# Slots of 1024 rows in the middle chunks of a convolution with a routed feed-forward network

## The chip, the cores and the metric

One core of one Trainium2 chip runs the kernel. The metric is the device time of one execution in microseconds (us); the median of three runs of the kernel before is 1307.97 us, with 1307.63 and 1311.01 as the others.

## The reference

```python
w = softmax(weight)                                  # 8 heads x 7 taps
x = causal convolution of x[8, 3584, 192] along the sequence, 24 columns per head
logits = x @ w_gate + modality_bias[modality_id]     # 28672 rows, 8 experts
e = argmax(logits, axis=1);  gate = softmax(logits)[e]
out[row] = gate * (relu(x[row] @ w1[e]) @ w2[e])     # w1 192x1024, w2 1024x192
```

With the inputs given, the rows go to three of the eight experts: 14239 to expert 6, 13901 to expert 7, 532 to expert 1.

## The kernel before, in words

The rows are worked off in two streams that run beside each other.

**Groups.** Nineteen groups (1, 1, 2, 2, 2 and then fourteen times 4 quads of 448 rows) are convolved, gated and sorted by expert. `convolve` (L264) multiplies with band matrices on TensorE (PE) and copies the result into one of four y buffers (two of them for a group of 4 quads); `turn`, `part_turned`, `gate`, `logits` and `choose` (L294 to L359) make the logits and the choice; `place` (L361) computes each row's place in a list of its expert in DRAM (`routed_rows`); `send` and `scatter` (L390, L210) write the rows there by one indirect DMA per 112 rows, issued by GpSimd (POOL). In `choose`, an iota on POOL (L357) writes the rows' own numbers into column 1 of y, so it has to wait until the earlier scatters out of that y buffer have landed. The first five groups (8 quads, 32 scatters) come before any expert work: this is the head.

**Slots.** A slot is a piece of one expert's list: 512 rows, or 256 in the last chunk. `Slot.__init__` (L605) loads the expert's weights on SyncE's (SP's) queue unless they are the same as two slots ago, `split` (L646, helper L98) turns them into a high and a low part, eight parts per slot, each with one copy on ScalarE (ACT, L99) and one subtraction on VectorE (DVE, L100). `bring` (L625) loads the slot's rows into one of two buffers. A pass is 256 rows: `turn` (L656) transposes them; four steps follow, each with `first` (L678, ten matmuls, relu on ACT and DVE) and, two steps later, `second` (L693, sixteen matmuls); `put` (L716) scales the result into two `o` tiles on DVE and scatters them to `out` by two indirect DMAs on POOL (L723). There are `OUTS` = 5 `o` buffers.

**Order.** `run` (L810) writes the order out by hand: step by step it emits `first`, `second`, some of the parts into which the group work is cut (as many as `due`, L775, asks for), a piece of the slot table of the next chunk, the loads and the splits of the next slot (eight parts over the eight steps of a slot). A chunk's slots may start only when its groups have been sent, and `due` aims at eleven steps before that. ACT keeps exactly this order; on the other engines a scheduler moves instructions that its model sees ready. There are 4 + 7 x 7 slots of 512 rows and a last chunk of up to 21 slots of 256, of which 8 always run: 61 slots, 114 passes, 456 steps. Before the last table is made, `fill` (L590) writes rows of zeros behind each expert's list, and `make_filler` (L580) writes the dummy list at the start, by DMAs on the ACT queue.

Of the kernel before, what the change touches and what calls it, by code (L numbers as in the profile page):

```python
# [9 lines left out]
F32 = mybir.dt.float32  # L10
# [16 lines left out]
WARM = 50  # L27
WARM2 = 0
WAIT = 3
OUTS = 5  # L30
PIN = 18
AHEAD = 26
T = 256
GROUPS_OF_CHUNK = (5, 2, 2, 2, 2, 2, 2, 2, 0)
SLOTS_OF_CHUNK = (4, 7, 7, 7, 7, 7, 7, 7)
PASSES_OF_SLOT = (2, 2, 2, 2, 2, 2, 2, 2, 1)
LEAD = 11
TURN = 1
LAG = 2
# [4 lines left out]
def conv_then_routed_ffn(ctx, tc, x, weight, modality, w_gate, mod_bias, w1, w2, out):  # L44
# [15 lines left out]
    W = D + OVER  # L60
    WIDE = max(PASSES_OF_SLOT)
    TW = WIDE * T
    CAP = N + TW
    DUMMY = E * CAP
    assert NJ == 2 and NG == sum(GROUPS_OF_CHUNK) and sum(QUADS_OF_GROUP) == 2 * NSB and NB == 8 and DB == 64 and CAP < 32768 and N % TW == 0
# [142 lines left out]
        return y_bufs[turns["y"] % 4]  # L208

    def scatter(chunk, idx, src):  # L210
        routed(chunk, nc.gpsimd.indirect_dma_start(  # L211
            out=scr, out_offset=bass.IndirectOffsetOnAxis(ap=idx, axis=0), in_=src, in_offset=None,
        ).ins)

    def routed(chunk, ins):
        for c in range(chunk + 1):
# [5 lines left out]
    class Group:  # L222
# [109 lines left out]
        def choose(self):  # L332

            n = self.tiles
            lg = self.lg

            def per_tile(ap):
                return ap.unsqueeze(2).broadcast_to([MB, n, E])

            top = rt.tile([MB, NT], F32, name="top")[:, 0:n]  # L340
            nc.vector.tensor_reduce(out=top, in_=lg, axis=AX.X, op=ALU.max)
            ex = rt.tile([MB, NT, E], F32, name="ex", bufs=1)[:, 0:n]
            nc.vector.tensor_tensor(out=ex, in0=lg, in1=per_tile(top), op=ALU.subtract)
            nc.scalar.activation(out=ex, in_=ex, func=AF.Exp)
            self.oh = rt.tile([MB, NT, E], BF16, name="oh")[:, 0:n]
            rk = rt.tile([MB, NT, E], F32, name="rk", bufs=1)[:, 0:n]
            nc.vector.tensor_tensor(out=rk, in0=lg, in1=per_tile(top), op=ALU.is_equal)
            nc.vector.tensor_tensor(out=rk, in0=rk, in1=ramp.unsqueeze(1).broadcast_to([MB, n, E]), op=ALU.mult)
            first = rt.tile([MB, NT], F32, name="first")[:, 0:n]
            nc.vector.tensor_reduce(out=first, in_=rk, axis=AX.X, op=ALU.max)  # L350
            nc.vector.tensor_tensor(out=self.oh, in0=rk, in1=per_tile(first), op=ALU.is_equal)
            den = rt.tile([MB, NT], F32, name="den")[:, 0:n]
            nc.vector.tensor_reduce(out=den, in_=ex, axis=AX.X, op=ALU.add)
            nc.vector.tensor_scalar(out=den, in0=den, scalar1=1e-9, scalar2=None, op0=ALU.add)
            for i, y in enumerate(self.ys):
                nc.vector.reciprocal(out=y[0:MB, 0:self.nb, 0], in_=den[:, i * self.nb:(i + 1) * self.nb])
                nc.gpsimd.iota(y.bitcast(I32)[0:MB, 0:self.nb, 1], pattern=[[S, self.nb]],  # L357
                               base=self.b0 * S + (self.block + i) * MB + MB - 1,
                               channel_multiplier=-1)  # L359

        def place(self):  # L361

# [117 lines left out]
    def init_tables():  # L480
        base0 = const.tile([1, E], F32, name="base0")
        nc.vector.tensor_copy(out=base0, in_=carry[0:1, :])
        done = const.tile([1, E], F32, name="done0")
        nc.vector.memset(done, 0.0)
        n_max = sum(n for _, n, *_ in plan)
        slot = const.tile([1, n_max], F32, name="slot")
        nc.gpsimd.iota(slot, pattern=[[1, n_max]], base=0, channel_multiplier=0,
                       allow_small_or_imprecise_dtypes=True)
        eid = const.tile([1, E], F32, name="eid")
        nc.gpsimd.iota(eid, pattern=[[1, E]], base=0, channel_multiplier=0,  # L490
                       allow_small_or_imprecise_dtypes=True)
        one8 = const.tile([1, E], F32, name="one8")
        nc.vector.memset(one8, 1.0)
        used = const.tile([1, n_max + 2], F32, name="used")
        nc.vector.memset(used[:, 0:2], -1.0)
        state.update(base0=base0, done=done, slot=slot, eid=eid, one8=one8, used=used)

    def table(chunk):

        s0, n, size = plan[chunk]  # L500
        last, down = chunk == len(plan) - 1, chunk % 2 == 1
        carry = state["carry"] if last else state["end", chunk]

        def small(name, shape=(1, E), dtype=F32):
            return rt.tile(list(shape), dtype, name=name, bufs=1)

        def wide(name):
            return rt.tile([1, n, E], F32, name=name, bufs=1)

        V = nc.vector  # L510
# [32 lines left out]
        V.tensor_tensor(out=past, in0=cmp, in1=state["eid"].unsqueeze(1).broadcast_to([1, n, E]), op=ALU.mult)  # L543
        used = state["used"]
        V.tensor_reduce(out=used[:, s0 + 2:s0 + 2 + n], in_=past, axis=AX.X, op=ALU.add)
        yield

        off = small("off")
# [10 lines left out]
        yield  # L559
        tab = rt.tile([1, n, 3], I32, name="tab")  # L560
        V.tensor_scalar(out=tab[:, :, 0], in0=row, scalar1=float(DUMMY), scalar2=None, op0=ALU.add)
        V.tensor_copy(out=tab[:, :, 1], in_=used[:, s0 + 2:s0 + 2 + n])
        V.tensor_tensor(out=past[:, :, 0], in0=used[:, s0 + 2:s0 + 2 + n], in1=used[:, s0:s0 + n], op=ALU.not_equal)
        V.tensor_tensor(out=tab[:, :, 2], in0=past[:, :, 0], in1=live, op=ALU.mult)
        yield
# [36 lines left out]
    class Slot:  # L602


        def __init__(self, i, chunk, ent):  # L605
            self.i, self.h, self.passes = i, {}, plan[chunk][2] // T
            self.chunk, self.ent, load = chunk, ent, nc.sync
            with tc.issue_after(state["load"]) if "load" in state else nullcontext():
                e = load.value_load(ent[:, 1:2], min_val=0, max_val=E - 1)
# [12 lines left out]
            if i > 0:  # L622
                load_second()

        def bring(self):  # L625
            chunk, size = self.chunk, plan[self.chunk][2]
            with tc.issue_after(state["load"]):
                r0 = nc.sync.value_load(self.ent[:, 0:1], min_val=0, max_val=DUMMY)
            self.rows = ring(sp, 2, [P, WIDE * NJ, W - DB], F32, "rows")[:, 0:size // P]
            self.ends = ring(sp, 2, [P, WIDE, NJ, DB], F32, "ends")[:, 0:size // T]  # L630
            src = scr[bass.ds(r0, size), :].rearrange("(j p) w -> p j w", p=P)
            for dst, part in ((self.rows, src[:, :, 0:W - DB]), (self.ends.rearrange("p k j d -> p (k j) d"), src[:, :, W - DB:W])):
# [9 lines left out]
            if self.i == 0:  # L642
                with tc.issue_after(ld):
                    self.load_second()

# [8 lines left out]
                split(w2b[i][:, cs, 0:D], w2b[i][:, cs, D:2 * D], raw2[i][:, cs, :])  # L654

        def turn(self, k):  # L656
            rows = self.rows[:, k * NJ:(k + 1) * NJ, :]
# [3 lines left out]
            nc.tensor.transpose(out=tp[:, NJ, :], in_=self.ends[:, k].rearrange("p j d -> p (j d)"), identity=ident)  # L661
# [107 lines left out]
    for c in range(1, last):  # L769
        steps += plan[c - 1][1] * steps_of(c - 1)  # L770
        g = sum(GROUPS_OF_CHUNK[:c + 1])
        marks.append((steps - LEAD, head + sum(parts_of(i) for i in range(FIRST, min(g + 1, NG)))
                      + (WAIT + 2 + 4 * QUADS_OF_GROUP[-1] if g == NG else 0)))

# [24 lines left out]
                pass  # L799
            made.append(Slot(len(made), chunk, tables[chunk][:, k, :]))  # L800

    def bring(i):

        make(i)
        while state["brought"] <= i:
            through("groups", order[state["brought"]][0])
            made[state["brought"]].bring()
            state["brought"] += 1

    def run(i0, i1):  # L810

        lagging, count = [], 0
        for i in range(i0, i1):
# [3 lines left out]
            for step in range(steps):  # L817
# [12 lines left out]
                if chunk < last and state["placed"] >= sum(GROUPS_OF_CHUNK[:chunk + 2]) and \  # L830
                        (chunk + 1 < last or state["groups"] == NG):
                    next(prepared.setdefault(chunk + 1, prepare(chunk + 1)), None)
                if steps == 4:
                    if step == 0:
                        bring(min(i + 2, i1 - 1))
                elif step == 0:
                    bring(min(i + 1, i1 - 1))
                    if i > i0:
                        make(min(i + 2, i1 - 1))
                elif step >= 4:  # L840
                    ahead = min(i + 2, i1 - 1)
                    if len(made) > ahead and state["groups"] >= sum(GROUPS_OF_CHUNK[:order[ahead][0] + 1]):
                        bring(ahead)
                    elif i == i0:
                        make(ahead)
                if i + 1 < i1:
                    if late:
                        parts = range(2 * step - 8, 2 * step - 6) if step >= 4 else ()
# [12 lines left out]
    def start(i):  # L861
        if i == 0:
            through("groups", 0)
            w2b.append(const.tile([P, NF, 2 * D], F32R, name="w2b1"))
        bring(i)
# [44 lines left out]
```

## Time and profile before

| | kernel before |
|---|---|
| median of three runs | 1307.97 us |
| the profiled execution | 1306.6 us |
| its span in the trace | 1304.9 us |
| PE / weight loads (PEld) / DVE / ACT / POOL busy | 1253.3 / 1222.3 / 1074.7 / 785.0 / 525.4 us |
| TensorE clock granted, mean | 0.983 |

The trace's times count from the span's start. The matmul times of the trace overlap one another, so a sum over a line is more than the engine's busy time; where matmuls follow one another without a gap, their starts tell how long one takes. Weight loads alternate with matmuls, and a stretch in which PEld is busy throughout is one in which PE is fed.

### The profile page before, as it was taken

How to read it: one execution, taken by the hardware profiler on the slowest of the kernel's cores; microseconds unless marked ns; L12 is line 12 of the kernel's file. 1: busy time of each engine (PE TensorE's matmuls, PEld its weight loads, DVE VectorE, ACT ScalarE, POOL GpSimd, SP SyncE). 2: the span in 40 equal slices, each digit the busy share in tenths (PEclk: the TensorE clock that was granted, in tenths of full speed). 3: DMA queues.
4: the chain of work that ended last, by engine and by line, in shares of the span. 5: the costliest groups of instructions: out<-in, count | busy, mean ns of one | idle time of the engine just before them, and what ended most of it. 6: DMA issues, size and time to landing. Idle time of an engine off the chain costs nothing.

```text
span 1304.9 us, 27875 instructions
## 1 busy us (share of the span) xinstructions
PE 1253.3 (96%) x9448; PEld 1222.3 (94%) x9448; DVE 1074.7 (82%) x2576; ACT 785.0 (60%) x1828; POOL 525.4 (40%) x574
## 2 busy tenths in 40 slices
PE   8549999999999999999999999999999999999997
PEld 7338899999999999999999999999999999999996
DVE  6459978798889888898889988898888878777895
ACT  2126566566666566766666566666665556555674
POOL 4636753442626244362624435262532612112121
PEclk9859999999999999999999999999999999999999
DMA  5467432352326241453215432352223525353440
GB/s 164 148 172 208 130 117 59 92 151 81 86 65 166 80 116 51 122 157 94 75 45 161 114 96 76 92 158 83 60 61 91 146 67 109 80 156 114 129 117 18
DMA packets 155356, 140.41 MB, mean 108 GB/s; under 512 B 43714, under 2 KB 141627, under 8 KB 155204
## 3 DMA queue, kind: packets, MB, share of 16 engines
q1 hardware_dynamic: 130164, 93.58, 27.3%
q0 software_dynamic: 23232, 44.30, 10.7%
q8 instruction: 76, 1.25, 0.4%
q10 hardware_dynamic: 1808, 0.66, 0.2%
q14 instruction: 76, 0.62, 0.2%
HBM read 160.37 MB, written 48.25 MB: 160 GB/s over the span
## 4 chain that ended last, share of the span: by engine, by line
PE 80%; issue 7%; DVE 6%; POOL 3%; DMA 2%; ACT 1%; POOLq 0%; DVEq 0%; ACTq 0%
PE hps L686 35%; PE po L704 23%; PE po L708 11%; PE cv L274 5%; PE gt L318 3%; POOL routed_rows L211 2%; PE tp L660 1%; DMA routed_rows<-y,idx 1%; POOL out_dram L723 1%; DVE hl L690 1%; PE hps L114 1%; PE tp L661 1%; DMA out_dram<-o,tag 1%; DVE turned L298 1%; DVE gx L100 1%
## 5 line engine op out<-in xcount | busy, mean ns | idle before, releaser
L704 PE MATMUL po<-w2b,hh 128*128 128x384 f32 x1824 | 555.5, 355 | 2.1 <-DVE o L722 1.7
L686 PE MATMUL hps<-sxh,w1b 128*128 128x256 f32 x1824 | 491.7, 292 | 0.5 <-ACT sxh L668 0.4
L689 ACT ACTIVATE hh<-hps 128x512 fp32r<-128x512 f32 x456 | 273.6, 600 | 349.0 <-PE hps L686 342.6
L723 POOL DMA_INDIRECT out_dram<-o,tag x228 | 237.2, 1040 | 530.4 <-DVE o L722 464.6
L708 PE MATMUL po<-w2b,hl 128*128 128x192 f32 x1824 | 440.6, 252 | 0.0
L690 DVE SCALAR_TENSOR_TENSOR hl<-hps,hh 128x512 fp32r<-128x512 f32 x456 | 312.8, 686 | 108.7 <-ACT hh L689 103.6
L686 PE MATMUL hps<-sxs,w1b 128*128 128x256 f32 x1824 | 362.7, 280 | 0.2 <-DVE sxs L670 0.2
L704 PEld LDWEIGHTS po<-w2b,hh 128*128 128x128 f32 x1824 | 343.6, 188 | 5.5 <-DVE o L722 4.8
L686 PEld LDWEIGHTS hps<-sxh,w1b 128*128 128x128 f32 x1824 | 345.0, 189 | 3.7 <-ACT sxh L668 0.6
L708 PEld LDWEIGHTS po<-w2b,hl 128*128 128x128 f32 x1824 | 345.2, 190 | 0.0
L211 POOL DMA_INDIRECT routed_rows<-y,idx x256 | 255.0, 996 | 143.8 <-issue 72.1
L686 PEld LDWEIGHTS hps<-sxs,w1b 128*128 128x128 f32 x1824 | 280.2, 189 | 0.4 <-issue 0.4
L686 PE MATMUL hps<-sxl,w1b 128*128 128x256 f32 x912 | 256.5, 281 | 3.1 <-DVE sxl L670 3.1
L100 DVE TENSOR_TENSOR w1b<-raw,w1b 128x512 fp32r<-128x512 f32 x244 | 164.9, 682 | 19.6 <-ACT w1b L99 17.3
L686 PEld LDWEIGHTS hps<-sxl,w1b 128*128 128x128 f32 x912 | 173.6, 190 | 5.6 <-DVE sxl L670 3.3
L99 ACT CAST w1b<-raw 128x512 fp32r<-128x512 f32 x244 | 149.0, 619 | 0.0
L100 DVE TENSOR_TENSOR w2b<-raw,w2b 128x384 fp32r<-128x384 f32 x244 | 133.0, 551 | 10.2 <-ACT w2b L99 10.0
L99 ACT CAST w2b<-raw 128x384 fp32r<-128x384 f32 x244 | 122.7, 511 | 0.0
L279 ACT COPY y<-cv 112x192 f32<-112x192 f32 (+1 forms) x198 | 53.7, 318 | 96.2 <-PE cv L274 72.3
L720 ACT ACTIVATE lowp<-po,tag 128x192 f32<-128x192 f32 x228 | 83.6, 418 | 31.2 <-PE po L704 31.2
L722 DVE SCALAR_TENSOR_TENSOR o<-po,tag,lowp 128x192 f32<-128x192 f32 x228 | 84.8, 411 | 5.4 <-ACT lowp L720 2.3
L274 PE MATMUL cv<-x,band 128*112 128x384 f32 (+2 forms) x160 | 47.7, 427 | 22.1 <-ACT y L279 19.6
(135 smaller groups left out, 1107.4 us busy)
## 6 DMA issues: line engine op xcount, KB each, us to landing
raw<-in_moe_w_dram SPq DMA_DIRECT2D x61, 768.0 KB
raw<-in_moe_w_dram SPq DMA_DIRECT2D x61, 512.0 KB
raw<-in_moe_w_dram SPq DMA_DIRECT2D x122, 256.0 KB
xr<-in_x_dram SPq DMA_DIRECT2D x36, 384.0 KB
rows<-routed_rows SPq DMA_DIRECT2D x53, 260.0 KB
x<-in_x_dram SPq DMA_DIRECT2D x26, 384.0 KB
ends<-routed_rows SPq DMA_DIRECT2D x53, 128.0 KB
routed_rows<-y,idx POOLq DMA_INDIRECT x256, 2.9
```

Source lines behind the costliest of these rows:

```text
L99: nc.scalar.copy(out=hi, in_=raw)
L100: return nc.vector.tensor_tensor(out=lo, in0=raw, in1=f(hi), op=ALU.subtract).ins
L211: routed(chunk, nc.gpsimd.indirect_dma_start(out=scr, out_offset=bass.IndirectOffsetOnAxis(ap=idx, axis=0), in_=src, in_offset=None,).ins)
L274: nc.tensor.matmul(cv, wt[:, h, :], xt[:, :, hs], start=n == 0, stop=n == len(terms) - 1)
L686: nc.tensor.matmul(hps[:, u, :], wa[:, c, fs], mv[z], start=n == 0, stop=n == len(terms) - 1)
L689: nc.scalar.activation(out=hh, in_=hps, func=AF.Relu)
L690: nc.vector.scalar_tensor_tensor(out=hl, in0=hps, scalar=0.0, in1=f(hh), op0=ALU.max, op1=ALU.subtract)
L704: nc.tensor.matmul(po, hh[:, u, js], wb[:, c, :], start=c == 0, stop=c == NF - 1, skip_group_check=True)
L708: nc.tensor.matmul(po[:, 0:D], hl[:, u, js], wb[:, c, 0:D], start=False, stop=False, skip_group_check=True)
L720: nc.scalar.activation(out=lowp, in_=po[:, D:2 * D], func=AF.Copy, scale=gate)
L722: nc.vector.scalar_tensor_tensor(out=o, in0=po[:, 0:D], scalar=gate, in1=lowp, op0=ALU.mult, op1=ALU.add)
L723: st = nc.gpsimd.indirect_dma_start(out=out, out_offset=bass.IndirectOffsetOnAxis(ap=tag.bitcast(I32)[:, j, 1:2], axis=0), in_=o, in_offse ...
```

## The change

The middle seven chunks get slots of 1024 rows (four passes, 16 steps) instead of 512, 23 of them in place of 42, and a chunk of three 512-row slots stands ahead of the last; 4 + 23 + 3 slots and 8 of 256 rows make 38 slots and again 114 passes. The weights of the next slot are split at every second step. The rows come in lots of 512, each in one of three buffers, and up to two lots ahead. Beside this, `OUTS` becomes 4, the iota of L357 has to follow the last scatter that was emitted before it on POOL, the filler pieces are as long as the widest slot (1024 rows, `TW` = `WIDE * T`), the last table lies in buffers of the input, and an empty slot's expert is -1 in the table, clipped to 0 for the load.

```diff
-OUTS = 5
+OUTS = 4
-GROUPS_OF_CHUNK = (5, 2, 2, 2, 2, 2, 2, 2, 0)
-SLOTS_OF_CHUNK = (4, 7, 7, 7, 7, 7, 7, 7)
-PASSES_OF_SLOT = (2, 2, 2, 2, 2, 2, 2, 2, 1)
+GROUPS_OF_CHUNK = (5, 2, 2, 2, 2, 2, 2, 2, 0, 0)
+SLOTS_OF_CHUNK = (4, 3, 3, 4, 3, 4, 3, 3, 3)
+PASSES_OF_SLOT = (2, 4, 4, 4, 4, 4, 4, 4, 2, 1)
...
+    LOT = 2
...
     def scatter(chunk, idx, src):
-        routed(chunk, nc.gpsimd.indirect_dma_start(
+        state["scatter"] = nc.gpsimd.indirect_dma_start(
...
-                nc.gpsimd.iota(y.bitcast(I32)[0:MB, 0:self.nb, 1], pattern=[[S, self.nb]],
+                with tc.issue_after(state["scatter"]) if "scatter" in state else nullcontext():
+                    nc.gpsimd.iota(y.bitcast(I32)[0:MB, 0:self.nb, 1], pattern=[[S, self.nb]],
...
-    def bring(self):
+    def bring(self, lot):
...
-        self.rows = ring(sp, 2, [P, WIDE * NJ, W - DB], F32, "rows")[:, 0:size // P]
-        self.ends = ring(sp, 2, [P, WIDE, NJ, DB], F32, "ends")[:, 0:size // T]
+        self.rows[lot] = ring(sp, 3, [P, LOT * NJ, W - DB], F32, "rows")[:, 0:(k1 - k0) * NJ]
+        self.ends[lot] = ring(sp, 3, [P, LOT, NJ, DB], F32, "ends")[:, 0:k1 - k0]
...
+    lots = [(i, lot) for i, (c, _) in enumerate(order) for lot in range(max(1, plan[c][2] // T // LOT))]
...
-                if steps == 4:
-                    if step == 0:
-                        bring(min(i + 2, i1 - 1))
-                elif step == 0:
-                    bring(min(i + 1, i1 - 1))
-                    if i > i0:
-                        make(min(i + 2, i1 - 1))
-                elif step >= 4:
-                    ahead = min(i + 2, i1 - 1)
-                    if len(made) > ahead and state["groups"] >= sum(GROUPS_OF_CHUNK[:order[ahead][0] + 1]):
-                        bring(ahead)
-                    elif i == i0:
-                        make(ahead)
+                if step == 0:
+                    make(min(i + 1, i1 - 1))
+                far = min(i + 2, i1 - 1)
+                if step >= (1 if late else 0) and order[far][0] in tables:
+                    make(far)
+                lot, end = lots.index((i, p // LOT)), sum(k < i1 for k, _ in lots) - 1
+                if min(steps, NF) - step % NF <= 6 or sent(min(lot + 1, end)):
+                    bring(min(lot + 1, end))
+                if state["brought"] > lot + 1 and sent(min(lot + 2, end)):
+                    bring(min(lot + 2, end))
```

## Rows read from the trace of the kernel before

**Rows 1.** Busy time by stretch: us, PE, PEld, DVE, ACT, POOL, clock, DMA share, GB/s

```profile
26.00:88.50 62.50, 33.48 (x165) 24.89 (x163) 30.40 (x129) 14.08 (x41) 34.33 (x44) 0.75 0.48 144
88.50:194.50 106.00, 98.04 (x676) 89.85 (x677) 94.08 (x245) 61.35 (x151) 65.51 (x67) 0.97 0.57 163
194.50:1005.30 810.80, 809.19 (x6220) 801.14 (x6219) 706.64 (x1626) 521.67 (x1200) 336.61 (x356) 1.00 0.35 97
1005.30:1216.20 210.90, 210.90 (x1654) 210.61 (x1652) 160.90 (x372) 123.80 (x286) 59.56 (x60) 1.00 0.41 110
1216.20:1295.20 79.00, 78.97 (x615) 78.61 (x613) 66.36 (x134) 55.95 (x127) 15.67 (x16) 1.00 0.36 103
```

**Rows 2.** The chain in time, two slots of 512 rows apart by one, no group work

```profile
1149.20 1.21 PE hps L686 x10
...
1168.37 1.21 PE hps L686 x10
```

**Rows 3.** Groups by line: what the splits cost

```profile
L100 DVE TENSOR_TENSOR w1b<-raw,w1b 128x512 fp32r<-128x512 f32 x244 | 164.9, 682 | 19.6 <-ACT w1b L99 17.3
L99 ACT CAST w1b<-raw 128x512 fp32r<-128x512 f32 x244 | 149.0, 619 | 0.0
L100 DVE TENSOR_TENSOR w2b<-raw,w2b 128x384 fp32r<-128x384 f32 x244 | 133.0, 551 | 10.2 <-ACT w2b L99 10.0
L99 ACT CAST w2b<-raw 128x384 fp32r<-128x384 f32 x244 | 122.7, 511 | 0.0
```

**Rows 4.** Waits on PE and PEld: us in total, times, longest us

```profile
PEld po L704 <- DVE o L722: 4.8, 13, 0.5
PE po L704 <- DVE o L722: 1.7, 8, 0.3
```

**Rows 5.** POOL's instructions in the head, in time: start, us, [idle before it]

```profile
26.08 1.13 POOL L211 DMA_INDIRECT routed_rows<-y,idx  x1 [1.61 <-ACT y L279]
...
37.17 0.94 POOL L211 DMA_INDIRECT routed_rows<-y,idx  x1 [0.30 <-issue]
38.13 0.32 POOL L288 TENSOR_TENSOR bt<-mt,step 112x64 f32<-112x64 f32 x1
38.53 0.32 POOL L291 TENSOR_TENSOR bt<-bt,both 112x64 f32<-112x64 f32 x1
43.39 0.14 POOL L357 IOTA y<- 112x8 int32 x1 [4.54 <-DMA routed_rows<-y,idx]
44.14 0.97 POOL L211 DMA_INDIRECT routed_rows<-y,idx  x1 [0.61 <-ACT y L279]
```

**Rows 6.** DVE in the head, in time: the places of the first and third group

```profile
24.96 0.16 DVE L384 CAST idx<-row 112x4 int32<-112x4 f32 x1
...
37.71 0.14 DVE L384 CAST idx<-row 112x8 int32<-112x8 f32 x1
```

**Rows 7.** ACT in the head, in time: copies that wait for y buffers

```profile
55.45 0.76 ACT L279 COPY y<-cv 112x192 f32<-112x192 f32 x3 [11.35 <-DMA routed_rows<-y,idx]
...
81.72 0.55 ACT L279 COPY y<-cv 112x192 f32<-112x192 f32 x2 [8.16 <-DMA routed_rows<-y,idx]
```

**Rows 8.** POOL around 400 us, in time: sixteen scatters of one group, then outputs

```profile
400.21 0.95 POOL L211 DMA_INDIRECT routed_rows<-y,idx  x1 [5.25 <-ACT hh L689]
...
419.44 1.26 POOL L211 DMA_INDIRECT routed_rows<-y,idx  x1 [0.30 <-issue]
420.71 0.16 POOL L357 IOTA y<- 112x8 int32 x1
421.04 1.01 POOL L723 DMA_INDIRECT out_dram<-o,tag  x1 [0.16 <-DVE take L573]
422.36 0.99 POOL L723 DMA_INDIRECT out_dram<-o,tag  x1 [0.30 <-DVE w1b L100]
```

**Rows 9.** DVE behind these outputs, in time

```profile
424.54 0.42 DVE L722 SCALAR_TENSOR_TENSOR o<-po,tag,lowp 128x192 f32<-128x192 f32 x1
425.78 0.42 DVE L722 SCALAR_TENSOR_TENSOR o<-po,tag,lowp 128x192 f32<-128x192 f32 x1 [0.83 <-DMA out_dram<-o,tag]
```

**Rows 10.** The filler's DMA issues: ns min/median/max, first and last start

```profile
L596 SPq DMA_DIRECT2D routed_rows<-filler x8: 372/373/414, 1072.7 to 1082.2; - x8
L585 ACTq DMA_DIRECT2D routed_rows<-filler x4: 339/444/471, 8.4 to 13.4; - x4
```

**Rows 11.** Busy time by stretch while the filler is written, columns as in rows 1

```profile
1075.00:1080.00 5.00, 5.00 (x42) 4.99 (x41) 3.64 (x10) 3.41 (x9) 1.57 (x2) 1.00 1.12 230
1080.00:1085.00 5.00, 5.00 (x41) 5.00 (x41) 4.09 (x13) 2.10 (x4) 0.37 (x1) 1.00 1.15 234
```

More of the change, by code (lines that the diff above doesn't have):

```diff
@@ L210, in scatter @@
     def scatter(chunk, idx, src):
-        routed(chunk, nc.gpsimd.indirect_dma_start(
+        state["scatter"] = nc.gpsimd.indirect_dma_start(
             out=scr, out_offset=bass.IndirectOffsetOnAxis(ap=idx, axis=0), in_=src, in_offset=None,
-        ).ins)
+        ).ins
+        routed(chunk, state["scatter"])
     def routed(chunk, ins):
@@ L356, in choose @@
                 nc.vector.reciprocal(out=y[0:MB, 0:self.nb, 0], in_=den[:, i * self.nb:(i + 1) * self.nb])
-                nc.gpsimd.iota(y.bitcast(I32)[0:MB, 0:self.nb, 1], pattern=[[S, self.nb]],
-                               base=self.b0 * S + (self.block + i) * MB + MB - 1,
-                               channel_multiplier=-1)
+                with tc.issue_after(state["scatter"]) if "scatter" in state else nullcontext():
+                    nc.gpsimd.iota(y.bitcast(I32)[0:MB, 0:self.nb, 1], pattern=[[S, self.nb]],
+                                   base=self.b0 * S + (self.block + i) * MB + MB - 1,
+                                   channel_multiplier=-1)
         def place(self):
@@ L489, in init_tables @@
         eid = const.tile([1, E], F32, name="eid")
-        nc.gpsimd.iota(eid, pattern=[[1, E]], base=0, channel_multiplier=0,
+        nc.gpsimd.iota(eid, pattern=[[1, E]], base=1, channel_multiplier=0,
                        allow_small_or_imprecise_dtypes=True)
@@ L501, in table @@
         last, down = chunk == len(plan) - 1, chunk % 2 == 1
-        carry = state["carry"] if last else state["end", chunk]
+        carry = state["carry"] if last else state["end", max(c for c in range(chunk + 1) if GROUPS_OF_CHUNK[c])]
         def small(name, shape=(1, E), dtype=F32):
@@ L507, in wide @@
         def wide(name):
+            if last:
+                return xp.tile([1, n, E], F32, name=name, tag=dict(cmp="xr_0", past="xr_1", of="xr_2")[name], bufs=1)
             return rt.tile([1, n, E], F32, name=name, bufs=1)
@@ L545, in table @@
         V.tensor_reduce(out=used[:, s0 + 2:s0 + 2 + n], in_=past, axis=AX.X, op=ALU.add)
+        V.tensor_scalar(out=used[:, s0 + 2:s0 + 2 + n], in0=used[:, s0 + 2:s0 + 2 + n], scalar1=-1.0, scalar2=None, op0=ALU.add)
         yield
@@ L561, in table @@
         V.tensor_scalar(out=tab[:, :, 0], in0=row, scalar1=float(DUMMY), scalar2=None, op0=ALU.add)
-        V.tensor_copy(out=tab[:, :, 1], in_=used[:, s0 + 2:s0 + 2 + n])
+        V.tensor_scalar(out=tab[:, :, 1], in0=used[:, s0 + 2:s0 + 2 + n], scalar1=0.0, scalar2=None, op0=ALU.max)
         V.tensor_tensor(out=past[:, :, 0], in0=used[:, s0 + 2:s0 + 2 + n], in1=used[:, s0:s0 + n], op=ALU.not_equal)
@@ L605, in __init__ @@
         def __init__(self, i, chunk, ent):
-            self.i, self.h, self.passes = i, {}, plan[chunk][2] // T
+            self.i, self.h, self.passes, self.rows, self.ends = i, {}, plan[chunk][2] // T, {}, {}
             self.chunk, self.ent, load = chunk, ent, nc.sync
@@ L623, in __init__ @@
                 load_second()
-        def bring(self):
+        def bring(self, lot):
             chunk, size = self.chunk, plan[self.chunk][2]
+            k0, k1 = lot * LOT, min(lot * LOT + LOT, self.passes)
             with tc.issue_after(state["load"]):
                 r0 = nc.sync.value_load(self.ent[:, 0:1], min_val=0, max_val=DUMMY)
-            self.rows = ring(sp, 2, [P, WIDE * NJ, W - DB], F32, "rows")[:, 0:size // P]
-            self.ends = ring(sp, 2, [P, WIDE, NJ, DB], F32, "ends")[:, 0:size // T]
-            src = scr[bass.ds(r0, size), :].rearrange("(j p) w -> p j w", p=P)
-            for dst, part in ((self.rows, src[:, :, 0:W - DB]), (self.ends.rearrange("p k j d -> p (k j) d"), src[:, :, W - DB:W])):
+            self.rows[lot] = ring(sp, 3, [P, LOT * NJ, W - DB], F32, "rows")[:, 0:(k1 - k0) * NJ]
+            self.ends[lot] = ring(sp, 3, [P, LOT, NJ, DB], F32, "ends")[:, 0:k1 - k0]
+            src = scr[bass.ds(r0, size), :].rearrange("(j p) w -> p j w", p=P)[:, k0 * NJ:k1 * NJ, :]
+            for dst, part in ((self.rows[lot], src[:, :, 0:W - DB]), (self.ends[lot].rearrange("p k j d -> p (k j) d"), src[:, :, W - DB:W])):
                 ld = nc.sync.dma_start(out=dst, in_=part).ins
@@ L641, in bring @@
             state["load"] = ld
-            if self.i == 0:
+            if self.i == lot == 0:
                 with tc.issue_after(ld):
@@ L656, in turn @@
         def turn(self, k):
-            rows = self.rows[:, k * NJ:(k + 1) * NJ, :]
+            lot, k0 = divmod(k, LOT)
+            rows = self.rows[lot][:, k0 * NJ:(k0 + 1) * NJ, :]
             tp = ring(ps_t, 4, [P, NJ + 1, P], F32, "tp", "t")
@@ L660, in turn @@
                 nc.tensor.transpose(out=tp[:, j, :], in_=rows[:, j, 2:2 + P], identity=ident)
-            nc.tensor.transpose(out=tp[:, NJ, :], in_=self.ends[:, k].rearrange("p j d -> p (j d)"), identity=ident)
+            nc.tensor.transpose(out=tp[:, NJ, :], in_=self.ends[lot][:, k0].rearrange("p j d -> p (j d)"), identity=ident)
             xh = ring(sp, 2, [P, NJ, P], F32R, "sxh")
@@ L771, in conv_then_routed_ffn @@
         g = sum(GROUPS_OF_CHUNK[:c + 1])
+        if not GROUPS_OF_CHUNK[c]:
+            break
         marks.append((steps - LEAD, head + sum(parts_of(i) for i in range(FIRST, min(g + 1, NG)))
@@ L800, in make, with bring, sent @@
             made.append(Slot(len(made), chunk, tables[chunk][:, k, :]))
[L802 to L807, printed above, removed]
+    lots = [(i, lot) for i, (c, _) in enumerate(order) for lot in range(max(1, plan[c][2] // T // LOT))]
+    def bring(n):
+        while state["brought"] <= n:
+            i, lot = lots[state["brought"]]
+            make(i)
+            through("groups", order[i][0])
+            made[i].bring(lot)
             state["brought"] += 1
+    def sent(n):
+        i, _ = lots[n]
+        return len(made) > i and state["groups"] >= sum(GROUPS_OF_CHUNK[:order[i][0] + 1])
     def run(i0, i1):
@@ L864, in start @@
             w2b.append(const.tile([P, NF, 2 * D], F32R, name="w2b1"))
-        bring(i)
+        bring(lots.index((i, 0)))
         for part in range(4 if i == 0 else 8):
```

## The prediction

> **What bounds the kernel now.** I read the busy time by stretch first, then the chain in time, the groups by line, the timelines of POOL, DVE and ACT, and the waits. By stretch [rows 1], PE is fed without a break from 194.5 us to the end of its work: its weight loads fill 801.14 of 810.80 us while group work runs beside the slots, and 210.61 of 210.90 after that. Without group work two passes take 1168.37 - 1149.20 = 19.17 us [rows 2], a pass 9.585, a step 2.40; 114 passes make 1092.7 us, and no edit changes that number or a matmul. So there are only three places where time can be won. One is the head: from 26 to 88.5 us PE works 33.48 of 62.50 us and at a granted clock of 0.75 of full speed. One is the first chunk, 88.5 to 194.5 us, where weight loads fill 89.85 of 106.00 us and DVE is at 94.08. The last is what is missing in the long middle: 9.66 us of PEld, against 0.29 of 210.90 in the stretch without groups, which over 810.80 us would be 1.1; 8.5 us are the most that a lighter DVE and ACT can give back there.
>
> **The change part by part**, against the profiled execution's own 1306.6 us (1304.9 of span and 1.7 around it); the median of the runs is 1.4 us above it.
>
> *Splits.* Each slot makes four parts of w1b and four of w2b; 61 slots made 244 of each, 38 make 152. DVE loses 92 x (682 + 551) ns = 113.4 us and ACT 92 x (619 + 511) = 104.0 us [rows 3]. DVE is at 87% in the middle stretch and would be at 73%, ACT at 64% and then 52%; but PE, not DVE, ends that stretch, so most of this is time off the path. The gain lies between 0 and the 8.5 us above. The waits of PEld and PE name o (L722) as what PE waits for [rows 4], 4.8 us on PEld, and these have to do with buffers, not splits; that leaves 3.7, of which I take 2.7. The first chunk keeps its 512-row slots and its eight splits in eight steps; nothing is won there.
>
> *The iota.* This is the part that I expect to count. In the head POOL stands from 38.85 to 43.39 us, 4.54 us, at an iota that waits until the second group's scatters have landed, and only then does it begin the third group's eight scatters, at 44.14 [rows 5]. The places of that group had been ready since 37.85 [rows 6]. In the first group it took from 25.12 (places ready) to 26.08 (first scatter), 0.96 us [rows 5, 6], so the third group could have begun at 38.81, 5.3 us earlier. Its y buffer is what ACT waits for, idle for 11.35 us until 55.45, and the same pattern with the fifth group's buffer lets ACT go on at 81.72, 8.16 us late [rows 7]; behind that stand the first slot's rows and the first step at 88.5. With the edit, an iota comes behind the scatters emitted before it, when its buffer has long been free, and all of this moves up together: -5.3 us. Bounds: 0, if something else is as late, and 7, if PE's reduced clock recovers with it. On POOL the moved iotas cost 0.14 us each before their own group's scatters; the scatters of one group wait for it and the outputs queued behind them, in a queue that is idle over half of the middle stretch (336.61 of 810.80 busy [rows 1]): nothing.
>
> *Four o buffers.* The scatters of a group go out as a batch of sixteen, from 400.21 to 420.70 us, and the outputs of a pass stand behind it; the first is issued at 421.04, the second 1.32 later [rows 8]. With five buffers the second o of the pass two later needs the first output's buffer: it starts at 425.78, 4.74 us after the issue, having waited 0.83 [rows 9]. With four, the first o needs that buffer, which then starts up to 1.24 us later than its 424.54, and the second waits for the second output, 1.3 us more than now. Behind o on DVE stand the low part of h and the splits, and PE waits for the bank that o empties. Fourteen groups have such a batch. Bounds: 0 and 14 x 1.3 = 18.2 us. Groups now take 24 or 32 steps in place of 28, all whole passes, so a batch should fall at about the same place in a pass as now, and of the waits that this gives today the longest is 0.5 us [rows 4]; nearest to these I take 0.35 us in half of the batches, +2.5 us.
>
> *Fillers.* Four more DMA issues on ACT's queue at the start, 444 ns each [rows 10], at most 1.8 us ahead of the first copies, partly under the wait for the bands: +0.5, between 0 and 1.8. The eight filler pieces before the last table double, from 3.2 to 6.4 MB (1024 rows of 776 B each); at the 230 to 234 GB/s that ran while they were written [rows 11] that is about 27 us on the queues behind SP, with the row and weight loads of the next slots queued behind. They stand at the beginning of a chunk of three slots, 24 steps or 57 us long, so the cost is 0 by that cover; if the weights of a slot eight steps later (19 us) were behind all of it, with 7 us for themselves, PE would lose about 15.
>
> *Loads.* Rows still come as 53 loads of 512 and 8 of 256; with three buffers a lot is asked for up to two lots, 16 steps or 38 us, ahead. SP waits longer at no load than at present: a weight load waits for splits that were emitted the slot before, now spread over 38 us. What is queued behind these on SP are the loads of x for the next group; the price is 0 unless a table comes late, and a table still follows the placing of its last group by some nine steps, over ten steps before its first weights are split. The group work of two groups has 48 or 64 steps for 56: in the shorter chunks DVE's group work per step rises by 56/48, and the splits' fall outweighs it.
>
> Sum: -5.3 - 2.7 + 2.5 + 0.5 = **-5.0 us**: 1301.6 for the profiled execution, and from the median **1303.0 us**.
>
> **The rivals.** *B, the head does not move*: another thing is as late as POOL there, or the scheduler finds a new order in which a different wait takes the iota's place; the edit then does nothing for the time. For it: POOL is not the only engine in that chain, and the loads and copies between the groups move too. Against it: the stall of 4.54 us is followed without a gap by scatters and by the waits of ACT. Then -2.7 + 2.5 + 0.5 = +0.3, 1308 us. *C, the fourth buffer decides*, and the kernel is slower: if in every group the first output behind a batch is issued less than 4.7 us before the o that needs its buffer, each of the fourteen batches costs 1.3 us on DVE at L722 and PE stands for it: 18.2 - 5.3 - 2.7 + 0.5 = +10.7, 1319 us. For it: the wait exists today, at 0.83 us; against it: only part of the batches show it. The Trainium skill, in Perfetto Trace Analysis, Optimization Strategy, says that one gap which keeps coming back on the engine that should be full can mean too few buffers; by that rule taking one away is the wrong way, with C's time, and the trace agrees so far that o's wait is the one that recurs [rows 4]. *D, more is won*: the lighter DVE gives back all 8.5 us, the head 7, and o costs nothing: -8.5 - 7 + 0.5 = -15, 1293 us. Against it: most of what is missing in the middle has no split as its cause.
>
> **How the numbers follow.** Forecast 0.52, B 0.24, C 0.11, D 0.13. About 0.3%, 3.9 us, is what a measurement of this kernel can tell from no change, so faster means below 1304.0 and slower above 1311.9. The forecast's own range, with 0 to 3.7 for the splits, 0 to 5 for o and 3 to 7 for the head, is 1298 to 1307; it lies below 1304.0 in about four cases of five. Faster: 0.42 + 0.13 = 0.55; same: 0.10 + 0.24 = 0.34; slower 0.11. The range leaves out C and the far end of D: 1296 to 1311.
>
> **What would show it.** Right: in POOL's timeline the third group's scatters begin near 39 us and no iota waits for a scatter; the first step at L686 starts near 83 us; DVE is below 965 us and ACT below 690 with 152 splits of each kind; PE's stretch from the first step to the last is within 4 us of today's. Wrong on o: waits of DVE at L722 on the output DMA of over 5 us in total, with PE behind them. Wrong on the loads: PE waiting at the transposes (L660) at the start of a chunk, or DVE at a split for its weights, above all in the chunk of three slots behind the filler. Wrong as a whole: a first step still at 88 us, or a middle that gains or loses over 8 us.

## The result and the profile after

The kernel after takes 1296.2 us (1294.9 to 1297.3, four runs) where the kernel before, on the same chip, takes 1308.11: a ratio of 0.9903, interval 0.9891 to 0.9915, or -11.9 us. The forecast was -5.0 us: the sign held, and the range of 1296 to 1311 by 0.2 us at its very end; the forecast's own range of 1298 to 1307 and the size did not. The profiled execution takes 1294.9 us, its span is 1293.2, that is 11.7 below the span of before.

I cut both traces at the first matmul of the first step, at steps 32 and 336, and at the last step. First the kernel after, busy time by stretch (us, PE, PEld, DVE, ACT, POOL, clock, DMA share, GB/s):

```profile
81.59:186.52 104.93, 96.49 (x675) 88.95 (x676) 93.89 (x246) 62.16 (x152) 67.51 (x69) 0.98 0.62 176
186.52:993.29 806.77, 804.50 (x6221) 799.90 (x6219) 631.24 (x1517) 452.14 (x1047) 348.83 (x372) 1.00 0.35 101
993.29:1278.71 285.42, 285.42 (x2231) 284.90 (x2230) 209.44 (x466) 164.12 (x379) 57.86 (x59) 1.00 0.38 100
```

The same three stretches in the kernel before:

```profile
88.47:194.46 105.99, 98.02 (x676) 89.84 (x676) 94.07 (x245) 61.34 (x151) 65.50 (x67) 0.97 0.57 163
194.46:1005.30 810.84, 809.23 (x6220) 801.18 (x6219) 706.68 (x1626) 521.71 (x1200) 336.65 (x356) 1.00 0.35 97
1005.30:1290.36 285.06, 285.06 (x2233) 284.67 (x2231) 226.18 (x504) 178.87 (x410) 74.25 (x75) 1.00 0.40 109
```

The first step comes 6.9 us earlier, the first chunk is 1.1 us shorter, the middle 4.1, the end 0.4 longer. In the middle the weight loads, which the prediction read, were idle for 9.66 us before (810.84 - 801.18) and for 6.87 after (806.77 - 799.90): 2.8 of the 4.1 us are idle time that went. PE's own rows hide this: by them it was idle for 1.6 us before and 2.3 after, and its busy time fell from 809.23 to 804.50 us. The record of a matmul runs on past the start of the next (one by the low part of h is 0.25 us long, and where nothing is waited for the next starts 0.09 us after it), so the first part of a wait counts as busy; the waits for o, at the end of this section, are 3.5 us by the weight loads and 2.9 by the matmuls, and before 4.8 and 1.7 [rows 4].

The head, in POOL's timeline of the kernel after, beside [rows 5]:

```profile
35.95 0.17 POOL L360 IOTA y<- 112x8 int32 x1
...
38.44 0.97 POOL L212 DMA_INDIRECT routed_rows<-y,idx  x1 [1.67 <-issue]
...
60.08 0.17 POOL L360 IOTA y<- 112x8 int32 x1
61.45 0.97 POOL L212 DMA_INDIRECT routed_rows<-y,idx  x1 [0.30 <-issue]
```

and in ACT's, beside [rows 7]:

```profile
49.74 0.76 ACT L281 COPY y<-cv 112x192 f32<-112x192 f32 x3 [7.20 <-DMA routed_rows<-y,idx]
...
75.53 0.54 ACT L281 COPY y<-cv 112x192 f32<-112x192 f32 x2 [7.17 <-DMA routed_rows<-y,idx]
```

No iota waits for a scatter any more; the third group's scatters begin at 38.44 us for 44.14 (predicted 38.81), and both copies that waited come 5.7 and 6.2 us earlier. The splits, beside [rows 3], number 152 of each kind as predicted, with durations that are the same to 3 ns:

```profile
L101 DVE TENSOR_TENSOR w1b<-raw,w1b 128x512 fp32r<-128x512 f32 x152 | 102.5, 685 | 14.0 <-ACT w1b L100 11.9
L100 ACT CAST w1b<-raw 128x512 fp32r<-128x512 f32 x152 | 92.3, 620 | 0.2 <-DMA raw<-in_moe_w_dram 0.2
L101 DVE TENSOR_TENSOR w2b<-raw,w2b 128x384 fp32r<-128x384 f32 x152 | 82.6, 553 | 16.2 <-ACT w2b L100 16.2
L100 ACT CAST w2b<-raw 128x384 fp32r<-128x384 f32 x152 | 75.9, 512 | 0.0
```

PE's waits for o, beside [rows 4], have become fewer and longer:

```profile
PEld po L713 <- DVE o L731: 3.5, 3, 1.7
PE po L713 <- DVE o L731: 2.9, 3, 1.5
```

### The profile page after: what moved, and what is told of

It reads as the page before. It is cut to its first block, busy times and chain, and to the rows that moved or that the text cites. A ratio compares the mean times of both kernels' runs of the same rounds, so it can differ in the third digit from the quotient of the medians.

```text
span 1293.2 us, 27020 instructions
## 1 busy us (share of the span) xinstructions
PE 1247.0 (96%) x9448; PEld 1219.8 (94%) x9448; DVE 982.2 (76%) x2431; ACT 701.5 (54%) x1644; POOL 523.2 (40%) x574
## 4 chain that ended last, share of the span: by engine, by line
PE 80%; issue 9%; DVE 4%; POOL 4%; DMA 2%; ACT 1%; ACTq 0%; POOLq 0%; SPq 0%; DVEq 0%
PE hps L695 35%; PE po L713 23%; PE po L717 11%; PE cv L276 5%; PE gt L320 3%; POOL routed_rows L212 2%; PE tp L669 2%; POOL out_dram L732 2%; PE tp L670 1%; DVE hl L699 1%; DMA routed_rows<-y,idx 1%; DVE w1b L101 0%; DMA out_dram<-o,tag 0%; DVE turned L300 0%; DVE gx L101 0%
## 5 line engine op out<-in xcount | busy, mean ns | idle before, releaser
L101 DVE TENSOR_TENSOR w1b<-raw,w1b 128x512 fp32r<-128x512 f32 x152 | 102.5, 685 | 14.0 <-ACT w1b L100 11.9
L101 DVE TENSOR_TENSOR w2b<-raw,w2b 128x384 fp32r<-128x384 f32 x152 | 82.6, 553 | 16.2 <-ACT w2b L100 16.2
L100 ACT CAST w1b<-raw 128x512 fp32r<-128x512 f32 x152 | 92.3, 620 | 0.2 <-DMA raw<-in_moe_w_dram 0.2
L100 ACT CAST w2b<-raw 128x384 fp32r<-128x384 f32 x152 | 75.9, 512 | 0.0
L679 DVE TENSOR_TENSOR sxs<-tp,sxs 64x128 fp32r<-64x128 f32 x228 | 65.8, 289 | 3.1
```

The lines of the kernel that those rows point to most:

```text
L100: nc.scalar.copy(out=hi, in_=raw)
L101: return nc.vector.tensor_tensor(out=lo, in0=raw, in1=f(hi), op=ALU.subtract).ins
L679: turned = nc.vector.tensor_tensor(out=lo, in0=raw, in1=f(hi), op=ALU.subtract).ins
```

## The experiments

Nine of the eighteen runs fell in jobs in which the kernel before itself took 1534 to 1545 us, and these say little; the other nine stand beside a kernel before of 1306 to 1308 us and are told first. "Middle" is steps 32 to 336, "end" steps 336 to 455; idle is the middle less the busy time in it, of PE and of its weight loads (PEld).

| kernel | us | ratio (interval) | first step | middle: us; PE busy, idle; PEld busy, idle | end |
|---|---|---|---|---|---|
| before | 1308.1 | | 88.5 | 810.84; 809.23, 1.61; 801.18, 9.66 | 285.06 |
| e9: before, iota edit | 1302.11 | 0.9955 (0.994, 0.997) | 86.0 | 810.94; 809.33, 1.61; 801.37, 9.57 | 285.06 |
| e17: before, four o | 1315.73 | 1.0067 (1.0049, 1.0086) | 90.7 | 815.98; 810.45, 5.53; 801.52, 14.46 | 285.06 |
| e14: after, slots of before | 1308.21 | 1.0001 (0.999, 1.0011) | 81.6 | 818.08; 812.83, 5.25; 804.61, 13.47 | 286.54 |
| e12: after | 1296.16 | 0.9914 (0.9885, 0.9943) | 82.1 | 806.86; 804.51, 2.35; 800.01, 6.85 | 285.46 |
| e18: after, free iota | 1304.67 | 0.9979 (0.997, 0.9989) | 88.4 | 808.57; 805.46, 3.11; 800.11, 8.46 | 285.46 |
| e5: after, splits twice | 1300.74 | 0.9955 (0.9937, 0.9972) | 82.2 | 810.65; 807.28, 3.37; 800.63, 10.02 | 285.41 |
| e13: after, five o | 1293.18 | 0.9883 (0.9856, 0.9909) | 82.5 | 803.91; 803.91, 0.00; 799.93, 3.98 | 285.45 |
| e15: after, first chunk 1024 | 1298.86 | 0.9925 (0.9898, 0.9952) | 84.3 | 810.62; 808.86, 1.76; 804.57, 6.05 | 286.88 |
| e16: e15 with five o | 1299.87 | 0.9939 (0.9923, 0.9956) | 84.4 | 813.08; 810.02, 3.06; 805.94, 7.14 | 286.99 |

The first scatter begins at 25.8 to 26.3 us in most of these executions and at 27.8 to 28.1 in those of e9, e15, e16 and e17, so 2 us of their first steps lie ahead of any edit's work. In e9 this belongs to the execution, for e6, the same kernel, begins at 25.46; for the other three it is not shown. My theory 1, as the expectations number it, changed on the way: for e5 and e9 it is "the splits make the middle shorter, the iota the head".

**The iota alone (e9; e1 and e6 are the same kernel).**

```diff
...
+with tc.issue_after(state["scatter"]) if "scatter" in state else nullcontext():
     nc.gpsimd.iota(y.bitcast(I32)[0:MB, 0:self.nb, 1], pattern=[[S, self.nb]],
...
```

> The kernel before, with the iota's new place alone, by itself on its chip. Theory 1 (the head by the iota, the middle by the splits): first step near 82 us, 1201 to 1202 us from step 0 to step 455, 6 to 7 us faster than the kernel before. Theory 2 (the iota's place helps in the middle too): that stretch 3 us or more shorter, 10 us faster. If the first step stays at 88 us, the head's gain comes from another edit.

Measured: -5.5 us beside its own kernel before; from first scatter to first step 58.2 us (86.02 - 27.78) for 62.4 before; the first chunk is 0.4 us longer, middle and end as before to 0.1 us. So theory 1, if less than its 6 to 7 us: the edit gains in the head and nowhere else.

**The kernel after without it (e18; e2 and e7 are the same kernel).**

```diff
-with tc.issue_after(state["scatter"]) if "scatter" in state else nullcontext():
+if True:
```

> The kernel after without the order of the iota, nothing else. Theory 1 (all of the head's gain is the iota's place): the first step at 88 to 89 us and not at 82, and 6 to 7 us slower than the kernel after, some 1302.5 to 1303.5 us. Rival (another of the edits moved part of the head): a first step at 84 to 87 us, 3 to 5 us slower.

Measured: 8.5 us over the kernel after by the medians. POOL's timeline has the old wait again, and the first step is back at 88.4:

```profile
43.98 0.14 POOL L360 IOTA y<- 112x8 int32 x1 [5.05 <-DMA routed_rows<-y,idx]
44.73 0.97 POOL L212 DMA_INDIRECT routed_rows<-y,idx  x1 [0.61 <-ACT y L281]
```

From first scatter to first step it takes 62.2 us (88.42 - 26.21), as before, so no other edit moves the head by itself. Beside the iota's place something else does: these steps take 58.2 us in e9 and 55.6 to 56.2 in the kernel after, e12 and e13, and 55.8 in e14, so it is neither the slots nor the buffers of o; which of the other edits it is was not tested. The middle is 1.7 us longer as well, 1.6 of it idle weight loads (8.46 for 6.85), which the expectation had not: in this kernel the place of the iotas counts there too.

**Five o buffers (e13, beside the kernel after again as e12; e4, e8, e10 and e11 are the same kernel as e13).**

```diff
-OUTS = 4
+OUTS = 5
```

> The kernel after, unchanged, beside the next three, so that they can be compared with it on one chip. Every theory expects a ratio to the kernel before of 0.989 to 0.992 where that one runs in some 1308 us; where it runs in some 1534 us, as in several jobs so far, 0.996 to 0.998, as its variants did there.

> The kernel after with five o buffers. Theory 1 (head 6.9 us, splits 4 to 5 us, the fourth buffer costs nothing): the kernel after's time within 0.7 us, and waits of PE and PEld for o near 2.9 and 3.5 us. Theory 2 (the fourth buffer costs the predicted 2.5 us, and the splits gave back over 7): 2 to 3 us faster than the kernel after, the waits for o lower by that much.

Measured: 3.0 us faster than e12, so theory 2. The line of o in e12 (what DVE waited for there, who waited for it):

```profile
  DMA out_dram<-o,tag: 3.6, 3
...
  PEld po L713: 3.7, 3
  PE po L713: 3.0, 3
```

and in e13, where no wait of DVE for the output DMA is left:

```profile
  PEld po L713: 0.9, 1
  PE po L713: 0.7, 1
```

In the middle no idle PE is left, and 3.98 us of idle weight loads:

```profile
187.32:991.23 803.91, 803.91 (x6220) 799.93 (x6219) 631.04 (x1517) 452.23 (x1047) 347.96 (x371) 1.00 0.36 101
```

The predicted price of the fourth buffer, 2.5 us, is there. The kernel after with five o buffers, 1293.18 us, is the fastest of all that were run and beats both kernels.

**Four o buffers in the kernel before (e17).**

```diff
-OUTS = 5
+OUTS = 4
```

> The kernel before with four o buffers, nothing else. Theory 1 (a buffer less costs 2.5 to 4 us, as between four and five in the kernel after): 1310 to 1313 us where the kernel before runs in some 1308, the waits of PE and PEld for o up by that much. Rival (it costs only where slots of 1024 put the batches elsewhere): within 1 us of the kernel before.

Measured: +8.2 us. Of the trace's 9.1 (span 1314.0 for 1304.9), 2.3 lie ahead of the first step, of which 1.8 ahead of the first scatter; 1.6 in the first chunk; 5.1 in the middle, 4.8 of these idle weight loads. DVE waits for the output DMA 5.6 us, 5 times, for 2.1, 3 times, before, and PEld for o 9.7 us at 16 places for 4.8 at 13. Both theories miss. The price of one buffer depends on the slots around it: in the middle 2.9 us with long slots (the kernel after against e13), 5.1 with short ones; the 8.2 hold the 1.8 us ahead of the first scatter, which may be no price of the buffer.

**The slots of before in the kernel after (e14; e3 is the same kernel).**

```diff
-SLOTS_OF_CHUNK = (4, 3, 3, 4, 3, 4, 3, 3, 3)
-PASSES_OF_SLOT = (2, 4, 4, 4, 4, 4, 4, 4, 2, 1)
+SLOTS_OF_CHUNK = (4, 7, 7, 7, 7, 7, 7, 7)
+PASSES_OF_SLOT = (2, 2, 2, 2, 2, 2, 2, 2, 1)
```

(and `GROUPS_OF_CHUNK` likewise)

> The kernel after with the slots of before (512 rows, 61 slots, eight splits in eight steps); the iota, four o buffers, three row buffers and the other edits stay. Theory 1: the head stays at a first step near 81.6 us, and the steps from the first to the last take 1201 to 1203 us, as before (1201.9), so 4 to 5 us more than the kernel after. Theory 2 (the fourth buffer does cost 2.5 us): 1203.5 to 1206 us for these steps. Rival (the longer slots win by their loads and their order, not by fewer splits; the twice-made splits cost by themselves): under 1199.5 us.

Measured: 12.0 us over e12, as slow as the kernel before, with the head's gain kept. Its middle:

```profile
187.27:1005.35 818.08, 812.83 (x6220) 804.61 (x6219) 707.88 (x1631) 520.76 (x1200) 339.34 (x358) 1.00 0.34 96
```

Against e12 that is 11.2 us: 6.6 of idle weight loads (13.47 for 6.85) and 4.6 of busy ones for the same matmuls (804.61 for 800.01). Most of the second part is not the slots': the kernel before has the same slots, and its weight loads are busy for 801.18 us. Nor is it a wait: e14's matmuls lie further apart in the end too, where PE never waits (286.54 us for 285.46), and why was not found. From the first step to the last e14 takes 1210.3 us, over every theory's figure; less the wider spacing (804.61 - 801.18 and 1.1 us in the end) it would be some 1206, theory 2's figure, and the long slots are worth some 7.5 of the 12 us beside four buffers. This is an estimate from these rows.

**Each split made twice (e5).** The kernel after, with its slots and loads, but 244 splits of each kind, as before:

```diff
-parts = range(step * 8 // steps, (step + 1) * 8 // steps)
+parts = range(step * 8 // steps, max(step * 8 // steps + 1, (step + 1) * 8 // steps))
```

> The changed kernel with every part of the splits of the 1024-row slots made twice, so that DVE and ACT have the 488 splits of the kernel before and all else is as changed. Theory 1 (the middle's gain is the fewer splits): the stretch from step 0 to step 455 is 4 us longer than the changed kernel's 1197.1 us, time 1300 us. Theory 2 (it is the iota's place, or the loads): that stretch is within 1 us of 1197.1, time 1296 us. If this run's chip stalls the engines around the scatters as the last one did (1534 us for the kernel before in place of 1308), only the ratio to the kernel before tells: 0.993 for theory 1, 0.990 for theory 2.

Measured: 1300.74 us, 4.5 over the kernel after (5.4 over e12 by the ratios), so theory 1, and nearly all of it in the middle. First e12's middle, then e5's:

```profile
186.94:993.80 806.86, 804.51 (x6220) 800.01 (x6219) 630.95 (x1517) 452.27 (x1047) 348.75 (x372) 1.00 0.35 101
187.25:997.90 810.65, 807.28 (x6221) 800.63 (x6219) 708.82 (x1669) 525.09 (x1199) 350.74 (x371) 1.00 0.35 100
```

Of these 3.8 us 3.2 are idle weight loads (10.02 for 6.85) and 0.6 busy ones. So the splits cost by waits: in the middle PEld waits for o 4.3 us at 4 places for 2.8 at 2 in e12, and in the group work (`cv`) 0.8 us for DVE's part of x where it does not wait in e12; the rest are delays too short for that list. The other 7.5 us, between e14 and e5, which have the same number of splits, are in the middle 3.4 of idle weight loads and 4.0 of e14's busy ones. What in the short slots, beside the number of splits, makes the first of these was not separated.

**Long slots in the first chunk (e15, and e16 with five o buffers).**

```diff
-SLOTS_OF_CHUNK = (4, 3, 3, 4, 3, 4, 3, 3, 3)
-PASSES_OF_SLOT = (2, 4, 4, 4, 4, 4, 4, 4, 2, 1)
+SLOTS_OF_CHUNK = (2, 3, 3, 4, 3, 4, 3, 3, 3)
+PASSES_OF_SLOT = (4, 4, 4, 4, 4, 4, 4, 4, 2, 1)
...
-                if step == 0:
+                if step == (8 if chunk == 0 and i + 1 == plan[0][1] else 0):
...
-                    if late:
-                        parts = range(2 * step - 8, 2 * step - 6) if step >= 4 else ()
+                    if chunk == 0:
+                        parts = (step - 8,) if step >= 8 else ()
```

> The kernel after with two slots of 1024 rows in place of four of 512 in the first chunk, the splits of the next slot in the last eight of sixteen steps: 16 splits of each kind fewer in the first 32 steps, 9.9 us of DVE there. Theory 1 (where DVE is at 94 of 106 us, as in the first chunk, a split given back is time): 2 to 6 us faster than the kernel after, all of it in the first 32 steps (105.0 us now). Rival (the first chunk is held by PE's own group work and by the loads of x): within 1 us of the kernel after.

> The first chunk's two slots of 1024 rows (as in the run before) with five o buffers. If both edits add up: the first 32 steps near 102.7 us, the waits for o near 0.9 us, 3 us faster than with four buffers. The spacing of the matmuls where no group work runs differs from kernel to kernel (96 steps took 230.57 us in the kernel after, 231.66 in the run before): with the kernel after's spacing 1291 us, with the other 1296 us.

Measured: a miss. The first chunk goes as theory 1 has it, with DVE at 85.43 us for 93.88 in e12 and 102.66 us for 104.85:

```profile
84.26:186.92 102.66, 96.41 (x676) 89.57 (x676) 85.43 (x229) 54.69 (x136) 67.06 (x72) 0.98 0.58 164
997.54:1284.42 286.88, 286.88 (x2232) 286.39 (x2230) 209.32 (x466) 164.05 (x379) 57.88 (x59) 1.00 0.43 115
```

But e15 is 2.7 us slower than e12 (1298.3 to 1301.1 us for 1295.7 to 1299.3, four runs each) and e16 6.7 slower than e13, whose kernels they should have beaten. The second row says where: the end, in which every engine's instructions come in the order of e12, takes 286.88 us for 285.46, and the weight loads' busy time in the middle grows by 4.56 us (804.57 for 800.01), in about that proportion (1.42 x 304 / 119 = 3.6), while their idle time falls. The wider spacing, once more, and not a wait. In e16's trace there is one wait for o of 3.3 us on PEld beside it, in place of the expected 0.9; this execution took 1303.7 us, the other three 1298.4 to 1300.0.

**The other nine runs.** e1 to e4 came in one job, e6 to e8 in another, e10 and e11 alone, for which the same was expected as for e13.

> The kernel before, with the iota's new place alone. Theory 1 (the gains add up: head by the iota, middle by the fewer splits): first step near 82 us, the stretch from the first step to the last as long as before (1201.9 us from step 0 to step 455), time 1301 us. Theory 2 (the iota's place frees POOL in the middle too, and the splits give nothing): first step near 82, that stretch about 4 to 5 us shorter, time 1296 us.

> The changed kernel with the iota free to move, as before. Theory 1: first step back at 88 us, the stretch from step 0 to step 455 as in the changed kernel (1197.1 us), time 1303 us. Theory 2: first step at 88 us and the stretch back at about 1202 us, time 1308 us. If the place of the iota matters in the head only because POOL is late there, POOL idles at an iota for over 4 us around 40 us again.

> The changed kernel with the slots, chunks and passes of before (61 slots, 488 splits), all else as changed (iota, four o buffers, lots with three buffers, order of loads). Theory 1: the stretch from step 0 to step 455 is 4 to 5 us longer than in the changed kernel, time 1301 us. Theory 2: as the changed kernel, 1296 us. A third theory (the fourth o buffer does cost, and the splits hide it): 1303 us or more, with DVE waiting at L731 for the output's DMA.

> The changed kernel with five o buffers. By the prediction's term for o (+2.5 us) it gains 2.5 us, to 1293.7 us; if the fourth buffer costs nothing, it is at 1296 us within 1 us.

| kernel | us, beside a kernel before of | ratios |
|---|---|---|
| before, iota edit (e1, e6) | 1534.66, 1535.5 beside 1533.9, 1533.7 | 0.9998, 1.0017 |
| after, free iota (e2, e7) | 1530.44, 1529.16 beside the same | 0.9976, 0.9974 |
| after, slots of before (e3) | 1535.24 beside 1533.9 | 1.0014 |
| after, five o (e4, e8, e10, e11) | 1527.43, 1529.85, 1538.39, 1530.62 beside 1533.9, 1533.7, 1544.7, 1533.6 | 0.996, 0.9981, 0.9959, 0.9974 |

There the engines stand still for reasons that no semaphore of the program shows; PE's waits in e10:

```profile
PE hps L695 <- issue: 60.2, 51, 9.5
PE po L713 <- issue: 41.0, 38, 2.6
PE po L717 <- issue: 37.7, 30, 2.9
```

None of these rows is among PE's waits in the kernel after on the other chips. The order is the same in the first of these jobs (five buffers before free iota before the slots of before); in the second, five buffers and free iota are the same within their spread, and the iota's edit alone gains nothing in either. No size is taken from them.

## Why the prediction was wrong in size

Term by term, from the traces: the head gave -6.9 us (forecast -5.3), the first chunk -1.1 (put at nothing), the middle with five o buffers on both sides -6.9 (-2.7, the splits), the fourth buffer +2.9 there (+2.5), the end +0.4 (0), and the fillers nothing (+0.5): -11.6 of the trace's -11.7. Two workings of the prediction don't come out: the ends of its own bounds give up to 1310.5 and not 1307 (1308 - 3 + 5 + 0.5), and DVE and ACT are busy 982.2 and 701.5 us where it expected under 965 and 690, though the splits' records fell by 112.8 and 103.5 us, nearly as forecast: the records of one engine overlap (DVE's groups of the kernel before add up to 1169.4 us, and it is busy for 1074.7), so busy time falls by less. Of the signs named for a right forecast a third just fails as well: from the first step to the last it is 4.8 us less, not within 4.

**The iota: right, a little small.** The forecast had -5.3 us and the third group's scatters at 38.81; they begin at 38.44. The edit alone gives -5.5 us (e9); taken from the kernel after it costs 8.5 (e18). In the trace the first step moved by 6.9. What the step missed is the same wait once more: ahead of the fifth group another iota waited for a landing (0.58 us before it in POOL's timeline of the kernel before), and the gap on POOL there, 2.4 us, is 1.4 now. That -5.5 lies so near is in part luck: in e9's trace the edit alone shortens the way from the first scatter to the first step by 4.2 us, in the kernel after, with the other edits, it is 6.8.

**The splits: wrong, and this is the step that failed.** The forecast allowed 8.5 us in the middle, took 4.8 off because PEld's waits name o, "and these have to do with buffers, not splits", and kept 2.7. But these waits have to do with both. With five o buffers on both sides, the kernel before and e13, PEld waits for o 4.8 us at 13 places and 0.9 at one, its idle time in the middle is 9.66 us and 3.98, and the middle is 6.9 us shorter. Making the splits twice (e5) brings such waits back without touching a buffer. With four buffers idle is 14.46 us with short slots (e17) and 6.85 with long ones (e12). So the term should have kept what it took off. By what way the splits make o late, whether DVE alone or also the outputs' DMAs behind it, was not followed. The sentence "no edit changes that number or a matmul" fails too, by less: the weight loads of the middle are busy 801.18 us before, 799.90 after, 804.61 in e14.

To see whether running splits also slow the matmuls beside them, I took from the records, steps 32 to 336, the distance from each of a step's eighteen matmuls (ten of `first`, eight of `second`) to the next in the step. One is called late when it is over 25 ns more than 95 in 100 of the same pair need, and the time above that is added up:

| kernel | late matmuls | us late | sum of the 5168 distances less that, us |
|---|---|---|---|
| before | 43 | 6.3 | 674.8 |
| e12: after | 11 | 4.0 | 674.3 |
| e5: after, splits twice | 36 | 6.8 | 674.6 |
| e13: after, five o | 6 | 1.1 | 674.3 |
| e14: after, slots of before | 45 | 10.3 | 678.1 |

Five or six of the late ones stand at the second matmul of a step, in every kernel; the others are among the first four of a pass's first `second`, which needs the banks that o empties. With twice as many splits the distances less the late time stay as they are, to 0.05%. The Trainium skill, in SBUF — State Buffer, section "SBUF: two separate sides", says that TensorE, ScalarE and VectorE on its own ports never wait on one another; by that rule copies beside the matmuls should leave their spacing alone, and e5 agrees, with 674.6 us for 674.3.

**The o buffers: right in the wait, near in size by luck.** +2.5 us forecast, +3.0 measured (e12 against e13), through the wait that was named, o behind its output DMA, 3.6 us in e12 and none in e13. It comes at 3 places of about 1.2 us instead of 0.35 in half of fourteen batches. The bound on the other side, rival C's 18.2 us, was far off even in e17, where the price is higher.

**The fillers and loads: right at the cover, half a microsecond too much at the start.** The first scatter begins at 25.97 us for 26.08, so the added issues cost nothing. At the last table the doubled pieces make SP's issues longer, up to 3.0 us, as the line of L602 in the kernel after shows, and PE is busy in every one of the 285.42 us around them:

```profile
L602 SPq DMA_DIRECT2D routed_rows<-filler x8: 372/972/3027, 1118.4 to 1135.3; - x8
```

**The rivals.** B fell with the head. C's wait was there at a sixth of its price. D was nearest: its two terms, -8.5 and -7, with the forecast's own o and filler, give -12.5, and -11.9 was measured. I gave it 0.13 because most of what was missing in the middle had no split as its named cause; that it had o as its named cause did not make it free of the splits.

**What stays open**: why one kernel's matmuls lie up to 0.7% further apart than another's where neither has group work (285.06 to 286.99 us for the same steps), which edit beside the iota's moved the head, and what made the first chunk 1.1 us shorter.

## What to carry to other kernels

Where PE seems busy throughout, look at the idle time of its weight loads before calling a gain spacing: the records of matmuls hid some 0.2 us of each wait here, and the number of weight loads is fixed, so here a change in their busy time was mostly spacing and one in their idle time a wait. A wait that names a buffer is not free of the load on the engine that fills it. An instruction that waits for a DMA in the queue that issues the DMAs belongs ahead of that wait, as soon as its own buffer is free. Parts of a change that look independent need not be: one buffer less cost 3 us with long slots and 5 to 8 with short ones, so measure such a part in the kernel in which it is to stand.

## What the runs showed of the hardware

The spacing of the matmuls belongs to the kernel, not to the chip or the execution. The end takes 285.06 us in before, e9 and e17, 285.4 to 285.5 in the kernel after, e5, e12, e13, e18 and, in the other jobs, e4, e8, e10 and e11, and 286.5 to 287.0 in e14 to e16, though the granted clock is 1.00 in these rows and the TensorE work is the same in all.

In the jobs at 1534 us all that is lost between the first step and the last lies ahead of the last scatter into the experts' lists. e10, whose last scatter is issued at 1206.5 us, takes 1430.8 us from the first step to the last for 1194.2 in e13, the same kernel, while the first 96 steps of the end take 230.64 us beside 230.58. In e1, e3 and e6, with short slots, that scatter comes behind step 336, at 1239 to 1245 us, and their end takes 302 to 303 us. The engines stop while the rows are still being scattered; what stops them was not found.
